# Joining the key loads of three head pairs and copying a quarter half aside

## The chip, the cores and the metric

The kernel runs on one core of a Trainium2 chip. The metric is the device time of one execution in microseconds (us), as the median of several runs; lower is better. All times here are microseconds unless marked ns. Engine names are those of the profile: PE (TensorE), DVE (VectorE), ACT (ScalarE), POOL (GpSimd), SP (the queue that issues almost all transfers).

## The reference

One decode step of a transformer block: attention over a long cache, then a small MLP mixer. What matters here is the attention, whose cache is nearly all of the data:

```
x: [1, 1, 512]; k_cache, v_cache: [1, 8, 16384, 128]; 32 query heads, 8 key/value heads, all bf16
q = (layernorm(x) @ wq) as 32 heads of 128
scores = q . k * 128**-0.5      (4 query heads share one key head)
p = softmax(scores);  o = p @ v;  h = x + o @ wo
out = h + B(layernorm(h))       (B: layernorm, two small branches, gelu with w3 and w4)
```

With one position, the branch of B that shifts along the sequence contributes nothing, so w1 and w2 are not read; w3 and w4 are.

## The kernel before, in words

The key and the value cache are 33.6 MB each. The kernel walks over four **pairs** of key/value heads (`PAIRS = 4`, loop at L720). For a pair, each of the 128 partitions holds 256 cache rows of 128 numbers: 64 KB of keys and 64 KB of values, 8.4 MB over all partitions. There is one key buffer `kb_all` and one value buffer `vb` of that size, so a pair's data can only be loaded when the pair before has been read. The key buffer is used as two **halves**, `kb[0]` and `kb[1]` (L444), 32 KB a partition each.

Per pair:
- `clear` (L658, ACT) zeroes the score banks; L724 (DVE) copies the pair's queries to `qn`.
- For each half y, `transpose_keys` (L635, DVE) transposes the half from `kb[y]` into the buffer `kt`. A half has eight **pieces**; `cuts` says at which pieces an instruction starts: (0, 4) is two instructions of four pieces, (0, 1, 2, 4, 6) five of 1, 1, 2, 2, 2. Both halves use the same `kt`, so a piece of the second half can only be written when PE has read that piece of the first.
- `scores` (L646, PE) does four matmuls a piece into the score banks. PE waits for DVE piece by piece.
- `load_keys(j + 1, y)` (L465, SP) loads the half of the next pair into `kb[y]`, once DVE has read it.
- `softmax` (L662): maximum (DVE, L664), a small matmul (L667), the exponential (ACT, L675), and the transposes of the probabilities into `pt` (DVE, L679).
- `unread(16)` (L498, matmuls of L500) lets PE do matmuls whose result nobody reads, while it waits for the softmax.
- `values` (L682): 64 matmuls with the values as the moving operand; they need `pt` and the landed values. `gather` (L700) rescales and adds up the output (L706 to L714). Then `load_values(j + 1)` (L470) loads the next pair's values into `vb`.

Every transfer is issued from SP in the order of the program, so SP's order is wq (two loads), keys 0 (two halves), values 0, keys 1 (two), values 1, keys 2 (two), values 2, keys 3 (two), values 3, then the weights: wo (L743, two loads, into `kb[0]`), w3 (L747) and w4 in three loads (L750), both into `kb[1]`. Each waits on SP for its buffer. One DMA semaphore per name (`k0`, `k1`, `v`, ...) counts a load's landing, and a reader waits for the whole load.

After the last pair the attention output is multiplied with wo (L759), the second layernorm follows on DVE (L514 to L561, inverse roots without ACT), then w3 (L784), GELU (ACT, L796), transposes (L800), w4 (L807), the output casts (L814 on DVE, L815 on ACT) and the store (L817).

PE's program is a hand-built loop over pieces and pairs, with one wait on DVE's count per piece; `worth` in an operation is by how much it raises that count (the number of pieces of a transpose).

Of the kernel before, what the change touches and what calls it, by code (L numbers as in the profile page):

```python
# [7 lines left out]
BF16 = mybir.dt.bfloat16  # L8
I32 = mybir.dt.int32
# [341 lines left out]
NHC = FM // 128  # L351

WQ = 2048
WO = ((0, 20), (20, 32))
VP = 1

# [3 lines left out]
PAIRS = HKV // 2  # L360
RPARTS = 6
QPAD = 4 * 7
KP = 8 * DH
# [9 lines left out]
def bass_sequential_preLN__gqa_block_cached__mixer_s_mlp__decode_kernel(  # L373
# [13 lines left out]
    with ExitStack() as ctx:  # L387
        sb = lambda name, shape, dt: ctx.enter_context(nc.sbuf_tensor(name, shape, dt))
        ps = lambda name, shape, dt: ctx.enter_context(nc.psum_tensor(name, shape, dt))
        P = Program(nc, ctx)  # L390
# [52 lines left out]
        kb_all = sb("kb", [128, 256 * DH], BF16)  # L443
        kb = [kb_all[:, i * 128 * DH:(i + 1) * 128 * DH] for i in range(2)]  # L444
        vb = sb("vb", [128, 256 * DH], BF16)
        kt = sb("kt", [128, 128 * DH], BF16)
        wq_sb, wo_sb = vb, kb[0]
        w3_sb = kb[1][:, 0:NCH * FM].rearrange("p (k f) -> p k f", k=NCH)
        w4_sb = kb[1][:, NCH * FM:2 * NCH * FM].rearrange("p (m c) -> p m c", m=NHC)
# [9 lines left out]
        def load(name, dst, src, key, by="SP", also=()):  # L459
            P.op(by, lambda e: e.dma_start(dst, src), w=[key, *also], dma=name)  # L460

        def pair_rows(src, j):
            return src[0, 2 * j:2 * j + 2].rearrange("g (u t) d -> (g u) (t d)", u=64)

        def load_keys(j, y):  # L465
            n = 128 * DH
            load(f"k{y}", kb[y][:, :], pair_rows(A_k_cache, j)[:, y * n:(y + 1) * n], ("r", y, 0),
                 also=[("r", y, i) for i in range(1, RPARTS)])

# [15 lines left out]
        def dve(fn, r=(), w=(), bank=()):  # L485
            return P.op("DVE", fn, r, w, bank)

        def act(fn, r=(), w=(), bank=()):
            return P.op("ACT", fn, r, w, bank)
# [8 lines left out]
        def unread(times):  # L498
            field = qb[:, :, :, :].rearrange("p a j q -> p (a j q)")
            P.op("PE", lambda e: e.matmul(O_ps[1][:, :], field[:, 0:128], field[:, 0:512], start=True, stop=True),  # L500
                 r=["qb"], bank=[("O", 1)], times=times)

        def piece(cuts, m):
            return [lo <= m < hi for lo, hi in cuts].index(True)
# [42 lines left out]
        def inverse_roots(i, ns):  # L547
# [23 lines left out]
        load("wq0", wq_sb[:, 0:WQ], wq_in[:, 0:WQ], "wq0")  # L571
        load("wq1", wq_sb[:, WQ:NCH * HQ * DH], wq_in[:, WQ:NCH * HQ * DH], ("v", 0), also=[("v", x) for x in range(1, VP)])
        load_keys(0, 0)
        load_keys(0, 1)

        dve(lambda e: e.memset(mean4[:, :], -1.0 / (32 * D)), w=["mean4"])
        pool(lambda e: e.memset(ident_f[:, :], 0.0), w=["ident_f"])
# [6 lines left out]
            r=["ident_f", "x4"], w=["quarter"])  # L584
# [11 lines left out]
            r=["ident_f"], w=["row32"])  # L596
        dve(lambda e: e.tensor_reduce(maskdd[:, :], ident_f[:, :].rearrange("p (n d) -> p d n", d=4), AX.X, ALU.add),
            r=["ident_f"], w=["maskdd"])
# [3 lines left out]
        for z, src, key, of, n in ((zo, row32[:, :].rearrange("p (g n h) -> p g h n", g=2, h=REP), "zo", "row32", 4),  # L602
# [6 lines left out]
            r=["hT", (("st", 0), 0), (("st", 0), 6), "wq0"] + [("v", x) for x in range(VP)], w=["xn"])  # L609
# [3 lines left out]
        for i, key in enumerate(keys):  # L613
            P.part("query", i)
            for k in range(NCH):
                pe(lambda e, k=k: e.matmul(row[:, bass.ds(P.b + P.b0, 512)], copies(xn[:, k:k + 1], 128),  # L616
                                           wq_k[:, k, bass.ds(P.c + P.c0, REP * DH)], start=(k == 0), stop=(k == NCH - 1)),
                   r=["xn"], also=[("v", x) for x in range(VP)], w=["n" if key == "mn" else key], bank=[key])
        P.part()
        for g in range(2):  # L620
            half = banks[64 * g:64 * g + 64, PAIRS * g:PAIRS * g + PAIRS, :].rearrange("p j c -> p (j c)")
            for b in range(2):
# [3 lines left out]
                    r=["n" if x == "mn" else x for x in keys[PAIRS * g:PAIRS * g + PAIRS]], w=["qcol"],  # L626
# [5 lines left out]
                qcol[lo:hi, :, :, 0].rearrange("p n (j h) -> p n j h", h=REP)), r=["qcol"], w=["qb"])  # L632


        def transpose_keys(y, cuts):  # L635
            for t, n in zip(cuts, [b - a for a, b in zip(cuts, [*cuts[1:], 8])]):
                view = lambda x, t=t, n=n: x[:, :].bitcast(I32).rearrange("p (x l w) -> p x (l w)", x=2, l=64)[
                    :, :, t * 512:(t + n) * 512]
                P.op("DVE", lambda e, view=view: e.transpose(view(kt), view(kb[y])),  # L639
                     r=[("r", y, i) for i in range(RPARTS)], w=[("kt", t + i) for i in range(n)], worth=n)  # L640

        def key_piece(at, n):
            part = kt[:, :].rearrange("p (x f) -> p x f", x=2)[:, :, bass.ds(at, KP)]
# [76 lines left out]
        for j in range(PAIRS):  # L720
            P.part()
            clear()
            P.part("query", j)
            dve(lambda e, j=j: e.tensor_copy(qn[:, :, :], qb[:, :, j, :]), r=["qb", ("s", 0), ("s", 1)], w=["qn"])  # L724
            for y in range(2):
                P.part("half", j, y)
                transpose_keys(y, (0, 4) if j < PAIRS - 1 else range(8) if y else (0, 1, 2, 4, 6))
                scores(j, y)
                if j < PAIRS - 1:
                    load_keys(j + 1, y)  # L730
            P.part("middle", j)
            softmax(j)
            unread(16)
            sums(j)
            values(j)
            P.part("rest", j)
            gather(j)
            if j < PAIRS - 1:
                load_values(j + 1)
# [9 lines left out]
        for n, (lo, hi) in enumerate(W4):  # L749
# [4 lines left out]
            r=["o_m"], w=["o_f"])  # L754
        dve(lambda e: e.tensor_copy(o_b[:, :], o_f[:, :]), r=["o_f", ("r", 0, 0)], w=["o_b"])  # L755

        for r_ in range(32):
# [4 lines left out]
               r=["o_b"] + [("r", 0, n) for n in (piece(WO, r_),) if n], w=[("O", 0)], bank=[("O", 0)],  # L762
# [4 lines left out]
        for n in range(2):  # L767
            dve(lambda e, n=n: e.tensor_copy(osum[:, 256 * n:256 * n + 256], O_ps[0][:, 256 * n:256 * n + 256]),
                r=[("O", 0)], w=[("osum", n)], bank=[("O", 0)])
        for q in range(4):  # L770
            pe(lambda e, q=q: e.matmul(h_ps[32 * q:32 * q + 32, 0:128], copies(row32[:, 0:1], 32),
                                       osum[:, q * 128:(q + 1) * 128], start=True, stop=True),
               r=[("osum", q // 2), "row32"], w=[hkey], bank=[hkey])
# [4 lines left out]
            r=["hT", (S, 0)] + [("r", 1, 0)], w=["hc"])  # L778
# [3 lines left out]
        for k in range(NCH):  # L782
            for q in range(4):
                pe(lambda e, k=k, q=q: e.matmul(s_ps[32 * q:32 * q + 32, 0, 0:FQ], hc[:, k, :],  # L784
                                                w3_sb[:, k, q * FQ:(q + 1) * FQ], start=(k == 0), stop=(k == NCH - 1)),
                   r=["hc"] + [("r", 1, n) for n in (piece(W3, k),) if n], w=[("s", 0)], bank=[("s", 0)])
# [6 lines left out]
            r=["xs", (S, 6), "hr"], w=[hkey], bank=[hkey])  # L793
# [9 lines left out]
        for m in range(NHC):  # L803
            if m == 4:
                pe(None)
            for o in range(4):
# [3 lines left out]
                   r=[("hcol", 2 * m // NHC)] + [("r", 1, len(W3) + n) for n in (piece(W4, m),) if n],  # L810
                   w=[hkey], bank=[hkey])
# [7 lines left out]
             r=[("fin", 0), ("fin", 1)], w=["out"], dma="out")  # L819
# [32 lines left out]
```

## Time and profile before

| | us |
|---|---|
| time, median of 3 runs (lowest to highest) | 189.69 (189.59 to 189.78) |
| span of the profiled execution | 189.0 |
| PE / DVE / ACT busy | 128.6 / 116.8 / 13.7 |
| data moved | 79.19 MB, mean 419 GB/s over the span |

The span runs from the first to the last instruction of one profiled execution; the time of a run also holds what lies around it. In the rows of the profile a group is named by line, engine, operation, output<-input and count; the brackets in a timeline row give the idle time of the engine before the group and what ended it. "kb" is the key buffer, which the wo, w3 and w4 loads use later.

### The profile page before, as it was taken

The numbers are of one execution on the slowest core, as the hardware profiler recorded it, in microseconds if no ns is written. First come the engines' busy times: TensorE is split into PE (matmuls) and PEld (weight loads), VectorE is DVE, ScalarE is ACT, GpSimd is POOL, SyncE is SP. The second block draws the span as 40 slices with busy tenths as digits, with TensorE's granted clock in tenths as the row PEclk, the third lists the DMA queues.
The fourth block names the chain that finished last, engine by engine and source line by source line (L and its number), as shares of the span: only waits on it lengthen the run. The fifth ranks groups of instructions, "written<-read, shape, count | busy, mean of one in ns | idle before, by whom it ended". The sixth has DMA issues, their size and how long they took to land.

```text
span 189.0 us, 2407 instructions
## 1 busy us (share of the span) xinstructions
PE 128.6 (68%) x767; PEld 49.7 (26%) x767; DVE 116.8 (62%) x139; ACT 13.7 (7%) x21; POOL 4.6 (2%) x8
## 2 busy tenths in 40 slices
PE   0109804979699049796980597969829997885772
PEld 0103301423225014232250242322513332222221
DVE  5740699695350897954518969445179897523173
ACT  3000200000040000000400000004000000500012
POOL 8100000000000000000000000000000000000000
PEclk9999995899999958999998589999987999999999
DMA  6999999999799999997999999997999999799994
GB/s 239 455 416 444 444 444 444 444 444 444 340 437 444 444 555 444 416 416 305 416 444 444 409 479 444 444 444 333 444 444 437 520 416 416 333 429 427 431 412 178
DMA packets 2895, 79.19 MB, mean 419 GB/s; under 512 B 334, under 2 KB 462, under 8 KB 718
## 3 DMA queue, kind: packets, MB, share of 16 engines
q1 hardware_dynamic: 2886, 79.17, 97.9%
q8 instruction: 1, 0.02, 0.0%
q10 hardware_dynamic: 8, 0.00, 0.0%
HBM read 79.17 MB, written 0.00 MB: 419 GB/s over the span
## 4 chain that ended last, share of the span: by engine, by line
DMA 36%; DVE 29%; PE 29%; issue 4%; SPq 1%; DVEq 0%
DVE kt L639 24%; DMA kb<-in_A_k_cache_dram 15%; DMA kb<-in_B_w_dram 15%; PE banks L650 13%; DMA vb<-in_A_wq_dram 6%; PE banks L500 6%; PE banks L616 5%; PE banks L690 4%; DVE mx L664 1%; DVE od L709 1%; DVE qcol L623 1%; SPq L460 1%; PE banks L667 1%; PE banks L712 0%; DVE od L706 0%
## 5 line engine op out<-in xcount | busy, mean ns | idle before, releaser
L650 PE MATMUL banks<-kt,qn 128*128 x256 | 69.2, 411 | 26.7 <-DVE kt L639 25.9
L639 DVE STREAM_TRANSPOSE kt<-kb 128x4096 int32<-128x4096 int32 (+2 forms) x25 | 70.7, 2878 | 5.6 <-PE banks L650 4.3
L650 PEld LDWEIGHTS banks<-kt,qn 128*128 x256 | 26.1, 102 | 69.2 <-issue 53.4
L500 PE MATMUL banks<-qb 128*128 128x512 bf16 x70 | 25.5, 388 | 0.6
L690 PE MATMUL banks<-vb,pt 128*32 128x512 bf16 x256 | 14.7, 379 | 0.9 <-POOLq L482 0.9
L675 ACT ACTIVATE p_sb<-banks,bias 128x1024 bf16<-128x1024 f32 x4 | 4.5, 1113 | 132.9 <-DVE nmh L671 132.9
L664 DVE TENSOR_REDUCE mx<-banks 128x1 f32<-128x1024 f32 x4 | 4.9, 1224 | 14.2 <-PE banks L650 14.2
L616 PE MATMUL banks<-vb,xn 128*128 x32 | 8.9, 448 | 6.8 <-DVE xn L607 6.8
L679 DVE STREAM_TRANSPOSE pt<-p_sb 64x1024 bf16<-64x1024 bf16 x8 | 9.9, 1239 | 5.4 <-ACT p_sb L675 5.3
L500 PEld LDWEIGHTS banks<-qb 128*128 128x128 bf16 x70 | 6.7, 97 | 18.3 <-issue 18.1
L706 DVE TENSOR_SCALAR od<-banks,rowc 128x128 f32<-128x128 f32 x4 | 1.4, 351 | 14.4 <-PE banks L690 14.4
L690 PEld LDWEIGHTS banks<-vb,pt 128*32 128x32 bf16 x256 | 8.5, 97 | 5.2 <-POOLq L482 1.0
L623 DVE STREAM_TRANSPOSE qcol<-banks 64x1024 f32<-64x1024 f32 x4 | 4.8, 1228 | 7.1 <-PE banks L616 7.1
L616 PEld LDWEIGHTS banks<-vb,xn 128*128 128x128 bf16 x32 | 3.6, 111 | 11.7 <-issue 9.2
L667 PE MATMUL banks<-mxd,mean 128*128 128x128 f32 x8 | 2.0, 326 | 6.6 <-DVE mxd L665 6.6
L712 PE MATMUL banks<-od,zo 128*32 128x128 f32 x8 | 1.6, 285 | 6.5 <-DVE od L709 6.5
L659 ACT ACTIVATE banks<-mean 128x1024 f32<-128x1024 f32 x4 | 4.1, 1027 | 19.0 <-DVE qcol L623 18.9
L699 DVE RECIPROCAL den<-banks 32x1 f32<-32x1 f32 x4 | 0.6, 156 | 6.9 <-PE banks L697 6.9
L709 DVE SCALAR_TENSOR_TENSOR od<-banks,rowc,od 128x128 f32<-128x128 f32 x12 | 4.2, 351 | 0.4
L759 PE MATMUL banks<-kb,o_b 128*32 128x512 bf16 x44 | 3.3, 384 | 1.6 <-DVE o_b L755 1.1
L585 PE MATMUL banks<-x,quarter 4*128 4x128 bf16 x1 | 0.3, 281 | 5.4 <-DVE quarter L583 5.4
L583 DVE CAST quarter<-ident_f 4x128 bf16<-4x128 f32 x1 | 3.2, 3225 | 1.0 <-DMA x<-in_A_x_dram 1.0
(69 smaller groups left out, 39.6 us busy)
## 6 DMA issues: line engine op xcount, KB each, us to landing
kb<-in_A_k_cache_dram SPq DMA_DIRECT2D x8, 4096.0 KB, 27.6
vb<-in_A_wq_dram SPq DMA_DIRECT2D x1, 3584.0 KB, 11.7
kb<-in_A_wo_dram SPq DMA_DIRECT2D x1, 2560.0 KB, 26.1
kb<-in_B_w_dram SPq DMA_DIRECT2D x1, 1792.0 KB, 24.2
kb<-in_A_wo_dram SPq DMA_DIRECT2D x1, 1536.0 KB, 29.4
kb<-in_B_w_dram SPq DMA_DIRECT2D x1, 1024.0 KB, 26.3
kb<-in_B_w_dram SPq DMA_DIRECT2D x1, 640.0 KB, 27.4
vb<-in_A_wq_dram SPq DMA_DIRECT2D x1, 512.0 KB, 3.6
```

Source lines behind the costliest of these rows:

```text
L500: P.op("PE", lambda e: e.matmul(O_ps[1][:, :], field[:, 0:128], field[:, 0:512], start=True, stop=True), r=["qb"], bank=[("O", 1)], times= ...
L616: pe(lambda e, k=k: e.matmul(row[:, bass.ds(P.b + P.b0, 512)], copies(xn[:, k:k + 1], 128), wq_k[:, k, bass.ds(P.c + P.c0, REP * DH)], sta ...
L623: dve(lambda e, g=g, b=b, half=half: e.transpose(qcol[64 * g:64 * g + 64, 2 * b:2 * b + 2, :, :].rearrange("p e m u -> p (e m u)"), half.r ...
L639: P.op("DVE", lambda e, view=view: e.transpose(view(kt), view(kb[y])), r=[("r", y, i) for i in range(RPARTS)], w=[("kt", t + i) for i in r ...
L650: pe(lambda e, n=n: e.matmul(row[:, bass.ds(P.y, 512)], qn[:, n, bass.ds(P.q, 128)], key_piece(P.k, n), start=False, stop=(n == 3), skip_g ...
L659: act(lambda e: e.activation(s_all, copies(mean4[:, 0:1], 1024), ACTF.Identity, scale=0.0), r=["mean4", "p"], w=[("s", 0), ("s", 1)], **both)
L664: dve(lambda e: e.tensor_reduce(mx[:, :], s_all, AX.X, ALU.max), r=[("s", 0), ("s", 1)], w=["mx"], **both)
L667: pe(lambda e: e.matmul(m_ps[:, 0:128], mean4[:, :], mxd[:, :], start=True, stop=True), r=["mxd", "mean4"], w=["m"], bank=["mn"])
L675: act(lambda e: e.activation(p_sb[:, :], s_all, ACTF.Exp, bias=bias[:, 0:1], scale=float(SCALE), accum_out=acc[:, :]), r=[("s", 0), ("s", ...
L679: dve(lambda e, g=g: e.transpose(pt[64 * g:64 * g + 64, :, :, g, :], p_sb[64 * g:64 * g + 64, :]), r=["p"], w=["pt"])
L690: pe(lambda e, l=l, ct=ct, ch=ch: e.matmul(O_ps[0][32 * ct:32 * ct + 32, :], pt[:, l, ch, :, :].rearrange("p g u -> p (g u)"), tiles[:, l ...
L709: dve(lambda e, block=block, c=c: e.scalar_tensor_tensor(od[:, :], block, rowc[:, c:c + 1], od[:, :], ALU.mult, ALU.add), r=[key, "rowc", ...
```

## The change

The keys of pairs 0, 1 and 2 (`WHOLE = 3`) come in one load each, 64 KB a partition, into the whole of `kb_all`; pair 3 keeps its two halves. The next pair's joined load is issued after the second half's scores are set up, and it waits for every reader of both halves. So that it need not wait for the last transposes, ACT copies the last two pieces (`ASIDE = 2`) of the second half into a new buffer `aside` as soon as the keys have landed, and DVE transposes those two pieces from there. The cuts change: for pairs 0 to 2 the first half goes in 2, 2, 4 pieces and the second in 4, 2, 2; for pair 3 the first half goes in 2, 2, 4 (1, 1, 2, 2, 2 before) and the second in eight single pieces as before. `unread` does 13 matmuls instead of 16, in all four pairs.

```diff
+WHOLE, ASIDE = 3, 2
...
+        aside = sb("aside", [128, 2, ASIDE * KP], BF16)
...
         def load_keys(j, y):
             n = 128 * DH
+            if j < WHOLE:
+                load("k0", kb_all[:, :], pair_rows(A_k_cache, j), ("r", 0, 0),
+                     also=[("r", 0, i) for i in range(1, RPARTS)] + [("r", 1, i) for i in range(RPARTS)])
+                return
             load(f"k{y}", kb[y][:, :], pair_rows(A_k_cache, j)[:, y * n:(y + 1) * n], ("r", y, 0),
...
         load_keys(0, 0)
-        load_keys(0, 1)
...
+        def pieces(x, t, n):
+            return x[:, :].rearrange("p (x l) -> p x l", x=2)[:, :, t * KP:(t + n) * KP]
+
+        def put_aside():
+            act(lambda e: e.copy(aside[:, :, :], pieces(kb[1], 8 - ASIDE, ASIDE)),
+                r=[("r", 1, i) for i in range(RPARTS)], w=["aside"])
+
-        def transpose_keys(y, cuts):
+        def transpose_keys(y, cuts, from_aside=False):
             for t, n in zip(cuts, [b - a for a, b in zip(cuts, [*cuts[1:], 8])]):
-                view = lambda x, t=t, n=n: x[:, :].bitcast(I32).rearrange("p (x l w) -> p x (l w)", x=2, l=64)[
-                    :, :, t * 512:(t + n) * 512]
-                P.op("DVE", lambda e, view=view: e.transpose(view(kt), view(kb[y])),
-                     r=[("r", y, i) for i in range(RPARTS)], w=[("kt", t + i) for i in range(n)], worth=n)
+                of = aside[:, :, :] if from_aside and t == 8 - ASIDE else pieces(kb[y], t, n)
+                P.op("DVE", lambda e, of=of, t=t, n=n: e.transpose(pieces(kt, t, n).bitcast(I32), of.bitcast(I32)),
+                     r=["aside"] if from_aside and t == 8 - ASIDE else [("r", y, i) for i in range(RPARTS)],
+                     w=[("kt", t + i) for i in range(n)], worth=n)
...
             dve(lambda e, j=j: e.tensor_copy(qn[:, :, :], qb[:, :, j, :]), r=["qb", ("s", 0), ("s", 1)], w=["qn"])
+            if j < WHOLE:
+                put_aside()
             for y in range(2):
                 P.part("half", j, y)
-                transpose_keys(y, (0, 4) if j < PAIRS - 1 else range(8) if y else (0, 1, 2, 4, 6))
+                if j < WHOLE:
+                    transpose_keys(y, (0, 4, 8 - ASIDE) if y else (0, 2, 4), from_aside=y == 1)
+                else:
+                    transpose_keys(y, range(8) if y else (0, 2, 4))
                 scores(j, y)
-                if j < PAIRS - 1:
+                if j < PAIRS - 1 and (y or j + 1 >= WHOLE):
                     load_keys(j + 1, y)
             P.part("middle", j)
             softmax(j)
-            unread(16)
+            unread(13)
```

On SP the joined load of pairs 1 and 2 stands where the second half's load stood; the first half's load, which was issued between the halves, is gone. For pair 3 both halves are issued where they were. On ACT the copy stands between `clear` and the exponential of pairs 0 to 2.

## The prediction

> **What bounds the kernel now.** The page first: span, transfer queue, chain.
>
> ```profile
> span 189.0 us, 2407 instructions
> ...
> q1 hardware_dynamic: 2886, 79.17, 97.9%
> ...
> DMA 36%; DVE 29%; PE 29%; issue 4%; SPq 1%; DVEq 0%
> ```
>
> The transfer engines are busy for 97.9% of the span, so the 79 MB of loads set a floor and the engines work beside them. The span is 189.0; the median of the runs, 189.69, lies 0.7 above it, and I keep that 0.7 as what lies around the span.
>
> Next, when each load lands. The timeline of SP's queue gives the issue times, the page's view of transfers, asked for each issue's window, the time from issue to landing.
>
> ```profile
> 1.65 1.02 SPq L460 DMA_DIRECT2D kb<-in_A_k_cache_dram  x2
> 22.83 0.33 SPq L460 DMA_DIRECT2D vb<-in_A_v_cache_dram  x1
> 35.16 10.53 SPq L460 DMA_DIRECT2D kb<-in_A_k_cache_dram  x2
> 61.46 0.33 SPq L460 DMA_DIRECT2D vb<-in_A_v_cache_dram  x1
> ...
> 82.92 0.33 SPq L460 DMA_DIRECT2D kb<-in_A_k_cache_dram  x1
> ```
>
> ```profile
> kb<-in_A_k_cache_dram SPq DMA_DIRECT2D x1, 4096.0 KB, 30.2
> vb<-in_A_v_cache_dram SPq DMA_DIRECT2D x1, 28.9
> kb<-in_A_k_cache_dram SPq DMA_DIRECT2D x1, 4096.0 KB, 26.2
> kb<-in_A_k_cache_dram SPq DMA_DIRECT2D x1, 4096.0 KB, 25.8
> vb<-in_A_v_cache_dram SPq DMA_DIRECT2D x1, 29.1
> kb<-in_A_k_cache_dram SPq DMA_DIRECT2D x1, 4096.0 KB, 27.4
> vb<-in_A_wq_dram SPq DMA_DIRECT2D x1, 512.0 KB, 3.6
> ```
>
> A merged row ends with its last issue of 0.33, so the second key half of pair 0 goes out at 1.65 + 1.02 - 0.33 = 2.34 and lands at 2.34 + 30.2 = 32.5. In the same way: values of pair 0 at 51.7; key halves of pair 1 at 61.4 and 45.36 + 25.8 = 71.2; values of pair 1 at 90.6; second key half of pair 2 at 82.92 + 27.4 = 110.3. Loads land one behind the other; every load is issued long before the one ahead of it ends.
>
> Then what one pair costs the engines (pair 2 and the start of pair 3).
>
> ```profile
> 101.40 8.76 DVE L639 STREAM_TRANSPOSE kt<-kb 128x4096 int32<-128x4096 int32 x2
> 111.60 8.77 DVE L639 STREAM_TRANSPOSE kt<-kb 128x4096 int32<-128x4096 int32 x2 [1.43 <-PE banks L650]
> ...
> 124.68 1.22 DVE L664 TENSOR_REDUCE mx<-banks 128x1 f32<-128x1024 f32 x1 [4.31 <-PE banks L650]
> ...
> 128.65 2.49 DVE L679 STREAM_TRANSPOSE pt<-p_sb 64x1024 bf16<-64x1024 bf16 x2 [1.33 <-ACT p_sb L675]
> ...
> 136.35 0.35 DVE L706 TENSOR_SCALAR od<-banks,rowc 128x128 f32<-128x128 f32 x1 [3.35 <-PE banks L690]
> ...
> 138.74 0.32 DVE L724 COPY qn<-qb 128x624 bf16<-128x624 bf16 x1
> 139.59 8.95 DVE L639 STREAM_TRANSPOSE kt<-kb 128x1024 int32<-128x1024 int32 x5 [0.53 <-DMA kb<-in_A_k_cache_dram]
> ...
> 149.30 9.13 DVE L639 STREAM_TRANSPOSE kt<-kb 128x1024 int32<-128x1024 int32 x8 [0.76 <-DMA kb<-in_A_k_cache_dram]
> ```
>
> Pair 2 transposes from 101.4, although its second key half lands only at 110.3: the engines start each pair on its first half, ahead of the transfers. They need 139.06 - 101.4 = 37.6 a pair against some 39.1 for its 16.8 MB (71.2 to 110.3), and reach pair 3 half a microsecond before its first half lands (139.59). Only there, and at the end, do engines wait for data.
>
> The end of the timeline:
>
> ```profile
> 159.68 1.22 DVE L664 TENSOR_REDUCE mx<-banks 128x1 f32<-128x1024 f32 x1 [1.25 <-PE banks L650]
> ...
> 172.41 0.35 DVE L706 TENSOR_SCALAR od<-banks,rowc 128x128 f32<-128x128 f32 x1 [4.41 <-PE banks L690]
> ...
> 175.43 2.54 PE L759 MATMUL banks<-kb,o_b 128*32 128x512 bf16 x32 [1.05 <-DVE o_b L755]
> ...
> 178.46 0.83 PE L759 MATMUL banks<-kb,o_b 128*32 128x512 bf16 x12 [0.48 <-DMA kb<-in_A_wo_dram]
> ...
> 183.86 0.16 DVE L561 SCALAR_TENSOR_TENSOR st<-st,sti 128x2 f32<-128x2 f32 x1
> 184.24 0.85 ACT L796 ACTIVATE hg<-banks,st 128x224 bf16<-128x224 f32 x2 [0.76 <-PE banks L784]
> 185.28 1.05 DVE L800 STREAM_TRANSPOSE hcol<-hg 128x224 bf16<-128x224 bf16 x2 [0.78 <-DMA kb<-in_B_w_dram]
> ...
> 186.83 0.56 PE L807 MATMUL banks<-kb,hcol 128*32 128x128 bf16 x24 [0.20 <-DMA kb<-in_B_w_dram]
> 187.44 0.28 DVE L814 CAST fin<-banks 64x128 bf16<-64x128 f32 x1 [1.11 <-PE banks L807]
> ```
>
> From the end of the wo matmuls (178.46 + 0.83 = 179.29) everything is one chain that waits for weights at two places by tenths only. Its own length: to the inverse root 184.02 - 179.29 = 4.73; 0.2 until the GELU starts; half of its 0.85; the transposes 1.05; 28 of the last matmuls, some 0.65. That is 7.1, where 187.44 - 179.29 = 8.15 passed. So the engines have **1.05 of slack** against the loads at the end, no more.
>
> **The change part by part.** *The joined load.* One semaphore now speaks for both halves, so the first transpose of pairs 0 to 2, and on DVE the whole pair behind it, waits for the second half: pair 0 from its present start of 26.3 (behind the query) to 32.5, pair 2 from 101.4 to 110.3. SP issues two instructions fewer before values 0 and one fewer before values 1 and 2; none of those waits on them. Rows of 64 KB instead of 32 KB: keys took 71.2 - 51.7 = 19.5 and 110.3 - 90.6 = 19.7, values (already 64 KB a row) 51.7 - 32.5 = 19.2 and 19.4. The gain lies between nothing and 0.5 a load; the means differ by 0.3, with single landings scattering as much, so I take 0.2: 0.6 by pair 2. Its keys then land at **109.7**.
>
> *Release of the buffer.* The next pair's keys go out after the transpose of the second half's third quarter (pieces 4 and 5) and ScalarE's copy of its last. A four-piece transpose takes 4.4 by the row at 101.40; for two pieces and for the copy I use these groups:
>
> ```profile
> L639 DVE STREAM_TRANSPOSE kt<-kb 128x2048 int32<-128x2048 int32 x3 | 6.7, 2269 | 0.0
> ...
> L659 ACT ACTIVATE banks<-mean 128x1024 f32<-128x1024 f32 x4 | 4.1, 1027 | 19.0 <-DVE qcol L623 18.9
> ```
>
> The copy has 4096 elements a partition, so it lies between one L659 and four, 1.0 to 4.1; I take 4.1, since it moves four times the elements. It starts at the landing; the next thing on ScalarE is the exponential some 23 later. It ends 11 before DVE reaches the release and costs nothing; it would from 15 on.
>
> *The new cuts*, timed from the start u of a pair's transposes. PE's pace, from the chain, the timeline and the stretches:
>
> ```profile
> 106.02 5.46 PE banks L650 x16
> ```
>
> ```profile
> 120.54 4.11 PE L650 MATMUL banks<-kt,qn 128*128 x16 [0.21 <-DVE kt L639]
> ...
> 126.61 6.03 PE L500 MATMUL banks<-qb 128*128 128x512 bf16 x16
> ```
>
> ```profile
> 105.00:108.00 3.00, 1.98 (x5) 0.81 (x6) 3.00 (x2) 0.00 (x0) 0.00 (x0) 0.50 0.81 350
> ```
>
> Four pieces (16 matmuls) take 4.11, or 5.46 just after the long wait, where the granted clock is 0.50.
> - First half in 2, 2 and 4 pieces: DVE ends at 2.27 + 2.27 + 4.4 less overlaps, 8.85 (four-four takes 8.76, the finer cut at 139.59 8.95). PE now starts at u + 2.4 instead of u + 4.6 and has done four pieces at 2.4 + 5.5 = 7.9. DVE needs just those to be free, so its stall of 1.43 goes. PE takes pieces 4 to 7 from 9.0 to 13.1.
> - Second half: 8.85 + 4.4 = 13.25, release at 15.5, last piece from the side buffer at 17.7. What is late next is PE: eight pieces from 13.4 at 1.03 each, scores done at **u + 21.6**, against 124.68 - 101.49 = 23.2 now. Finer cuts at the end of the half bring nothing more.
> - Three warming matmuls fewer: 3 x 6.03 / 16 = 1.13. They end at 132.64 now, the transposed probabilities are there at 128.65 + 2.49 = 131.14, so all 1.13 counts.
> - From scores to the next pair's start 139.06 - 124.68 = 14.4 now, 13.25 then. A pair takes 21.6 + 13.25 = **34.85** instead of 37.6.
>
> *Does the queue stay full?* Pair 0 starts at 32.3, gives its buffer free at 47.8 and is done at 67.2. Pair 1 starts with its keys at 70.8, releases at 86.3, is done at 105.6. The wq row above (512 KB in 3.6, of which 1.2 is moving bytes at the values' 19.4 per 8.4 MB) gives at most 2.4 from issue to bytes at both ends. Values 0 land at 51.7 and values 1 at 90.2, so the keys have 1.5 to spare both times. Values of pairs 1 to 3 go out at u + 32.4, at least 3 before the keys ahead of them land.
>
> *The sum.* Pair 2 starts at 109.7 (8.3 later) and is done at 109.7 + 34.85 = 144.55. Keys of pair 3, still in halves, have landed by then (139.5 and 149.3 before), so pair 3 starts 5.0 later than at 139.59. Its first half again ends at u + 8.85; PE, empty from 7.9 to 9.0, then has twelve pieces in a row, 12.35 long, while DVE's eight single transposes take 9.13: scores done at u + 21.35 = 165.9, before 159.68. To the rescaling of the output 11.67 (136.35 - 124.68, with no wait for values) less 1.13: 176.45 against 172.41; here the wait for the last values has hidden part. Then 3.02 to wo and, with all of wo long landed, 2.54 + 0.83 = 3.37: wo ends at 182.85 against 179.29. The tail's own 7.1 leads to 189.95, where the output cast stood at 187.44. **+2.5**, a span of 191.5 and a time of 192.2.
>
> So the cover of the joined load is the start on half a pair: once it is gone, no pair can begin before its last byte, and from 109.7 on two pairs and the tail stand one behind the other, 80.2 long, where the loads after that point need only some 77.
>
> *A rule beside it.* The Trainium skill, TensorE: Matmul & The Clock Gate, in its part on the clock gate, says that the activity window is free-running and the number of slow matmuls changes from run to run. This trace has one phase only (the 0.50 row). By that rule PE could stay slow for up to two windows of 3.4 after its first matmul, an estimate from that page; four pieces would then end at u + 9.3 instead of 7.9.
>
> Apart from it, four pieces wholly at half clock (twice 4.11) would end at u + 10.6, a stall of 1.8 at most in pair 2; I take none, as the chain shows 5.46, and keep part of it in the range.
>
> **The rivals.**
> - *A dry queue.* If the copy does not free the buffer sooner (the change doesn't do what it says), release comes at u + 17.7: 50.0 and 88.5, about 0.7 inside the 2.4 each time. Keys 1 and 2 are late by 0 to 0.7 each, and pair 2 with them: 192.2 to 193.6. Against it: the copy's 4 lies far before 15.
> - *Faster, by fewer transfers.* If each load had a cost of its own of x that the next load does not cover, three joins bring pair 2's keys 3x earlier. 2.5 must be won over the 0.6 counted, so it decides from x = 1.0; at 2.4, the bound from the wq row, pair 2 starts at 103.1 and the time is 185.6. For it: nothing. Against it: halves land 71.2 - 61.4 = 9.8 apart, twice which is 19.6, and a single load of the same bytes takes 19.4.
>  The Trainium skill, DMA: Bandwidth & Descriptors, Anatomy of one DMA, gives each transfer a fixed cost of about 2.0; taken as x it would make an estimate of 186.8. The trace's 0.2 speaks against that for queued loads.
> - *Hidden anyway.* If the engines' chain were 2.5 shorter than summed (twenty matmul pieces at 0.9, say), the last weights would set the end again: 189.1 to 189.7. Pieces of 1.03 in every full-clock stretch speak against it.
>
> **How the numbers follow.** Forecast 0.79, own range 191.0 (0.4 a load) to 193.4 (no gain from longer rows, part of the slow-clock stall); dry queue 0.11; fewer transfers 0.04; hidden anyway 0.05, mostly within 0.2%; other 0.01. 0.2% is about what a measurement of this kernel can tell from no change. Predicted 192.2; range 190.9 to 194.2 (up to a dry queue with no gain from the rows), which leaves out the faster cases. Faster 0.06, same 0.04, slower 0.90.
>
> **What would show it.** Right: first transposes of pairs 0, 1 and 2 each right after a wait for keys, at about 32.3, 70.8 and 109.7; pair 3 waiting for PE's gather, not for data, near 144.5; no DVE wait on PE between the halves; the tail without waits for weights, its transfers done before its matmuls ask for them. Wrong: a transfer gap at 51 or 90 (dry queue), pair 2's keys before 107 (fewer transfers), or a last wait for w4 (hidden).

## The result and the profile after

The changed kernel takes **194.82** (median of 6 runs, 193.24 to 195.23) against 189.74 before (189.53 to 190.0): a ratio of **1.0259**, 95% interval 1.0241 to 1.0276. Ratios here and below are estimated over the runs and are not exactly the quotient of the two medians. The forecast was 192.2 with a range to 194.2; the direction and the path were right, but the forecast +2.5 is about half of the measured 5.1.

The page of the changed kernel, first its span, the transfer queue and the chain, then two groups (line, engine, operation, output<-input, count | busy, mean ns | idle before and its cause):

```profile
span 193.5 us, 2365 instructions
...
q1 hardware_dynamic: 2454, 79.17, 95.4%
...
DMA 40%; DVE 29%; PE 26%; issue 3%; SPq 0%; ACT 0%; DVEq 0%; ACTq 0%
DMA kb<-in_A_k_cache_dram 40%; DVE kt L650 23%; PE banks L662 13%; PE banks L506 5%; PE banks L702 4%; PE banks L776 2%; DVE mx L676 1%; DVE od L721 1%; PE banks L824 1%; PE banks L679 1%; PE banks L724 0%; SPq L462 0%; DVE od L718 0%; DVE hcol L817 0%; DVE mxd L677 0%
...
L650 DVE STREAM_TRANSPOSE kt<-kb 128x2048 int32<-128x2048 int32 (+2 forms) x26 | 63.9, 2524 | 14.3 <-DMA kb<-in_A_k_cache_dram 14.3
...
L644 ACT COPY aside<-kb 128x4096 bf16<-128x4096 bf16 x3 | 10.8, 3605 | 34.2 <-DMA kb<-in_A_k_cache_dram 34.2
```

The same bytes are moved, but the queue no longer fills the span (95.4% instead of 97.9%): the transfers are done before the end, and the last load of the weights is gone from the chain. It now runs through keys and transposes only. DVE waits 14.3 for keys, three times, where it waited 1.3 before. The copy takes 3.6 each time.

DVE's timeline, cut down to the points that the forecast named (start, duration, what ended the idle time before):

```profile
32.50 15.35 DVE L650 STREAM_TRANSPOSE kt<-kb 128x2048 int32<-128x2048 int32 x5 [5.72 <-DMA kb<-in_A_k_cache_dram]
...
72.00 15.39 DVE L650 STREAM_TRANSPOSE kt<-kb 128x2048 int32<-128x2048 int32 x5 [4.73 <-DMA kb<-in_A_k_cache_dram]
...
110.74 15.35 DVE L650 STREAM_TRANSPOSE kt<-kb 128x2048 int32<-128x2048 int32 x5 [3.84 <-DMA kb<-in_A_k_cache_dram]
...
132.31 1.23 DVE L676 TENSOR_REDUCE mx<-banks 128x1 f32<-128x1024 f32 x1 [4.03 <-PE banks L662]
...
145.38 17.84 DVE L650 STREAM_TRANSPOSE kt<-kb 128x2048 int32<-128x2048 int32 x11
...
166.90 1.22 DVE L676 TENSOR_REDUCE mx<-banks 128x1 f32<-128x1024 f32 x1 [3.68 <-PE banks L662]
...
177.35 0.35 DVE L718 TENSOR_SCALAR od<-banks,rowc 128x128 f32<-128x128 f32 x1 [3.35 <-PE banks L702]
...
191.98 0.28 DVE L831 CAST fin<-banks 64x128 bf16<-64x128 f32 x1 [0.68 <-PE banks L824]
```

Each joined pair begins right behind its wait for keys, the half-to-half stall on PE is gone (five transposes in a row), pair 3 waits for no data, and nothing in the tail waits for weights. Pair 2 starts 9.3 later than before (110.74 against 101.4) and everything behind it follows.

### The profile page after: what moved, and what is told of

Its sections match the earlier page's. It is cut to its first block, busy times and chain, and to the rows that moved or that the text cites. A ratio compares the mean times of both kernels' runs of the same rounds, so it can differ in the third digit from the quotient of the medians.

```text
span 193.5 us, 2365 instructions
## 1 busy us (share of the span) xinstructions
PE 127.6 (66%) x755; PEld 50.1 (26%) x755; DVE 116.8 (60%) x143; ACT 24.5 (13%) x24; POOL 4.6 (2%) x8
## 3 DMA queue, kind: packets, MB, share of 16 engines
q1 hardware_dynamic: 2454, 79.17, 95.4%
## 4 chain that ended last, share of the span: by engine, by line
DMA 40%; DVE 29%; PE 26%; issue 3%; SPq 0%; ACT 0%; DVEq 0%; ACTq 0%
DMA kb<-in_A_k_cache_dram 40%; DVE kt L650 23%; PE banks L662 13%; PE banks L506 5%; PE banks L702 4%; PE banks L776 2%; DVE mx L676 1%; DVE od L721 1%; PE banks L824 1%; PE banks L679 1%; PE banks L724 0%; SPq L462 0%; DVE od L718 0%; DVE hcol L817 0%; DVE mxd L677 0%
## 5 line engine op out<-in xcount | busy, mean ns | idle before, releaser
L662 PE MATMUL banks<-kt,qn 128*128 x256 | 71.7, 417 | 34.4 <-DVE kt L650 34.2
L650 DVE STREAM_TRANSPOSE kt<-kb 128x2048 int32<-128x2048 int32 (+2 forms) x26 | 63.9, 2524 | 14.3 <-DMA kb<-in_A_k_cache_dram 14.3
L506 PE MATMUL banks<-qb 128*128 128x512 bf16 x58 | 21.4, 425 | 0.4
L644 ACT COPY aside<-kb 128x4096 bf16<-128x4096 bf16 x3 | 10.8, 3605 | 34.2 <-DMA kb<-in_A_k_cache_dram 34.2
L702 PEld LDWEIGHTS banks<-vb,pt 128*32 128x32 bf16 x256 | 9.3, 97 | 3.4
L506 PEld LDWEIGHTS banks<-qb 128*128 128x128 bf16 x58 | 5.7, 99 | 15.0 <-issue 14.8
L650 DVE STREAM_TRANSPOSE kt<-aside 128x2048 int32<-128x2048 int32 x3 | 6.8, 2269 | 0.0
L671 ACT ACTIVATE banks<-mean 128x1024 f32<-128x1024 f32 x4 | 4.1, 1027 | 19.4 <-DVE qcol L628 19.3
L776 PE MATMUL banks<-kb,o_b 128*32 128x512 bf16 x44 | 4.5, 530 | 1.1 <-DVE o_b L772 1.1
```

The costliest lines, as they stand in the source:

```text
L644: act(lambda e: e.copy(aside[:, :, :], pieces(kb[1], 8 - ASIDE, ASIDE)), r=[("r", 1, i) for i in range(RPARTS)], w=["aside"])
L650: P.op("DVE", lambda e, of=of, t=t, n=n: e.transpose(pieces(kt, t, n).bitcast(I32), of.bitcast(I32)), r=["aside"] if from_aside and t == 8 ...
L662: pe(lambda e, n=n: e.matmul(row[:, bass.ds(P.y, 512)], qn[:, n, bass.ds(P.q, 128)], key_piece(P.k, n), start=False, stop=(n == 3), skip_g ...
L702: pe(lambda e, l=l, ct=ct, ch=ch: e.matmul(O_ps[0][32 * ct:32 * ct + 32, :], pt[:, l, ch, :, :].rearrange("p g u -> p (g u)"), tiles[:, l ...
L776: pe(lambda e, r_=r_, q=q: e.matmul(O_ps[0][32 * q:32 * q + 32, :], copies(o_b[:, r_:r_ + 1], 32), wo_sb[:, r_ * D:(r_ + 1) * D], start=(r ...
```

## The experiments

All diffs are against the changed kernel unless said otherwise; the ratios are against the kernel before. The theory: a joined pair cannot start before its last byte, and behind pair 2's last byte two pairs and the tail stand in series. The rivals: a dry transfer queue, the copy, the new cuts or the fewer warming matmuls, the 64 KB rows.

### The changed kernel again (e1_again)

> The changed kernel once more, to see which of its pieces repeat. My theory: pair 2 starts when its joined keys have landed (110 to 111 in the profile) and from there the engines set the end; spans fall into two groups near 191.9 and 193.5, the longer when the wo matmuls run partly at half clock. Rival (a dry transfer queue): the keys of pair 1 land late by about 0.8 every time, with stretched packets at their start, and this is the larger part of the excess over the forecast.

194.71 (ratio 1.0258, 1.0240 to 1.0277). Pair 2 starts at 111.16, wo takes 4.47. In this repeat pair 1 starts at 71.50, earlier than in the first profile, and pair 2 later: the lateness is there in both, but not at the same load. The spans lie between 192.9 and 193.8 here, so these four do not fall into the two groups that were expected. Single shorter runs exist all the same: one of the six above has a span of 191.9, and e5, e8, e9 and e13 each have one or two that are 1.2 to 1.6 below the next of the same kernel. None of these is a profiled run, so what they save is not shown.

### Which join costs (e3_whole2, e13_join_pair2)

```diff
-WHOLE, ASIDE = 3, 2
+WHOLE, ASIDE = 2, 2
```

> Only the keys of pairs 0 and 1 are joined. My theory: pair 1 starts at 71 to 72, pair 2 right behind it at 106 (its first half landed at 100.5), pair 3 at 141, 1.5 later than before; the tail's 1.05 of slack takes most of it: 189.7 to 190.6, the upper end if wo runs at half clock. Rival (each joined load costs alike, 5.1 / 3): 193.1.

190.30 (1.0035, 1.0017 to 1.0054). Two of the three joins cost 0.6 together. DVE in this kernel:

```profile
106.15 17.83 DVE L650 STREAM_TRANSPOSE kt<-kb 128x2048 int32<-128x2048 int32 x11
...
140.74 17.83 DVE L650 STREAM_TRANSPOSE kt<-kb 128x2048 int32<-128x2048 int32 x11
```

Pairs 2 and 3 start without a wait for data, right behind the pair before, and 34.6 apart.

The other way round, only pair 2's keys are joined:

```diff
-            if j < WHOLE:
+            if j == 2:
                 load("k0", kb_all[:, :], pair_rows(A_k_cache, j), ("r", 0, 0),
...
         load_keys(0, 0)
+        load_keys(0, 1)
...
-                if j < PAIRS - 1 and (y or j + 1 >= WHOLE):
+                if j < PAIRS - 1 and (y or j + 1 != 2):
```

> Only the keys of pair 2 are joined; pairs 0 and 1 come in halves. Theory (only the last join counts, since two pairs and the tail stand behind it, while pairs 0 and 1 have four spare microseconds each): pair 2 at 110 to 111, time 193.6 to 195, nearly as with three joins. Rival (each join costs alike): 191.4.

193.45 (1.0174, 1.0132 to 1.0217; a little below the forecast's lower end), with pair 2 at 109.98:

```profile
109.98 8.83 DVE L651 STREAM_TRANSPOSE kt<-kb 128x2048 int32<-128x2048 int32 x3 [12.88 <-DMA kb<-in_A_k_cache_dram]
```

DVE, which had reached pair 2 at 97, stands 12.88 until the last byte. This one join costs 3.7 of the 5.1, the other two alone 0.6. (The two do not add up to 5.1: in e13 the keys of pair 2 go out at 77.85, long before the values ahead of them land, and come without the lateness that is shown further down.) The joins do not cost alike: what counts is how much work stands behind the joined bytes.

### Start on half a pair (e4_halves_late, e11_late_first)

```diff
             if j < WHOLE:
-                load("k0", kb_all[:, :], pair_rows(A_k_cache, j), ("r", 0, 0),
-                     also=[("r", 0, i) for i in range(1, RPARTS)] + [("r", 1, i) for i in range(RPARTS)])
+                for h in range(2):
+                    load(f"k{h}", kb[h][:, :], pair_rows(A_k_cache, j)[:, h * n:(h + 1) * n], ("r", h, 0),
+                         also=[("r", h, i) for i in range(1, RPARTS)])
                 return
```

> Keys of pairs 0 to 2 again in two loads with a semaphore each, but both issued at the joint late release, and the last two pieces still copied aside; DVE starts on the first half. My theory (the wait for the last byte costs): pair 0 starts at 26.8, pair 2 at its first half near 100.5, the time is 189.3 to 190.0. Rival (late issue, or the copy on ScalarE, costs): 192 to 195.

189.69 (1.0001, 0.9991 to 1.0011). The run was not quite what was meant: the first half's load waits only for its own readers and, for pair 1, went out at 35.8, not with the second. A second version holds both back by an instruction on SP that waits for every reader of the buffer:

```diff
             if j < WHOLE:
+                if j:
+                    P.op("SP", lambda e: e.nop(), w=[("r", h, i) for h in range(2) for i in range(RPARTS)])
+                for h in range(2):
+                    load(f"k{h}", kb[h][:, :], pair_rows(A_k_cache, j)[:, h * n:(h + 1) * n], ("r", h, 0),
+                         also=[("r", h, i) for i in range(1, RPARTS)])
                 return
```

> The same two loads, both issued only when the whole buffer is free, but DVE starts a pair on its first half. Theory (the wait for the last byte is the cost): pair 2 starts at its first half, near 100.3, and the time is 189.4 to 190.0. Rival (the late issue costs by itself): 191 or more.

189.60 (0.9996, 0.9986 to 1.0005), with every piece of the change but the join in place: the copy, the cuts, 13 matmuls, the joint release.

```profile
100.16 8.83 DVE L653 STREAM_TRANSPOSE kt<-kb 128x2048 int32<-128x2048 int32 x3 [3.07 <-DMA kb<-in_A_k_cache_dram]
...
138.96 8.83 DVE L653 STREAM_TRANSPOSE kt<-kb 128x2048 int32<-128x2048 int32 x3 [3.09 <-DMA kb<-in_A_k_cache_dram]
```

The pairs start with their first halves, ten before the joined load would have landed, and the loads set the end again. The shorter pairs (34.6 instead of 37.6) show as a wait of 3.1 for data, with another 0.9 between the halves, and gain nothing.

### The cuts and the matmuls without a join (e2_whole0, e12_before_cuts)

```diff
-WHOLE, ASIDE = 3, 2
+WHOLE, ASIDE = 0, 2
...
         load_keys(0, 0)
+        load_keys(0, 1)
```

> No load is joined and nothing is copied aside; the new cuts and the 13 warming matmuls stay. My theory: the join alone costs time, so the loads set the end again: 189.3 to 190.0, a pair 34.8 long, pair 3 waiting for its first half at about 139.5. Rival (the new cuts or the missing warming matmuls cost, by the clock or by more instructions): 191 or more.

191.88 (1.0120, 1.0103 to 1.0137), outside what the theory allowed. But its page begins

```profile
span 188.3 us, 2376 instructions
```

which is the span of the kernel before in its runs beside (188.1 to 188.8). The excess lies outside the span: 3.4 to 3.7 here, where every other kernel has 1.3 to 1.6. This run is also not quite what its expectation says: with `WHOLE = 0` every pair takes the cuts of pair 3, so all second halves go in eight single pieces. So the kernel before got the new cuts for pairs 0 to 2 ((0, 2, 4) and (0, 4, 6)), the new one for pair 3, and 13 matmuls:

```diff
-                transpose_keys(y, (0, 4) if j < PAIRS - 1 else range(8) if y else (0, 1, 2, 4, 6))
+                transpose_keys(y, ((0, 4, 6) if y else (0, 2, 4)) if j < PAIRS - 1 else range(8) if y else (0, 2, 4))
...
-            unread(16)
+            unread(13)
```

> The kernel before with the new cuts in all pairs and 13 warming matmuls; no join, no copy, no buffer for it. If the 2.2 that the version without any join took more than the kernel before lies in these cuts or in the fewer matmuls: 191 to 192 here too, with a span near 188.4. If it is a matter of that one program (its span was that of the kernel before, and the excess lay outside the span): 189.4 to 190.0.

189.64 (1.0000, 0.9989 to 1.0011). Cuts and matmuls cost nothing where the loads set the end. What lengthened that one program outside its span stays open.

### Is it one chain from pair 2 on? (e7_unread16)

```diff
-            unread(13)
+            unread(16)
```

> The changed kernel with 16 warming matmuls a pair instead of 13. My theory: from pair 2 on the engines are one chain, so it pays 1.13 twice, in pairs 2 and 3: 197.0. Rival (transfers set the end): no change, 194.8.

196.51 (1.0367, 1.0345 to 1.0389), 1.7 more than the changed kernel and not 2.2. The profile shows why:

```profile
110.10 15.35 DVE L650 STREAM_TRANSPOSE kt<-kb 128x2048 int32<-128x2048 int32 x5 [3.14 <-DMA kb<-in_A_k_cache_dram]
...
145.92 17.84 DVE L650 STREAM_TRANSPOSE kt<-kb 128x2048 int32<-128x2048 int32 x11
```

```profile
182.13 4.29 PE L776 MATMUL banks<-kb,o_b 128*32 128x512 bf16 x44 [1.05 <-DVE o_b L772]
```

Pair 2 happened to start at 110.10, 0.64 earlier. From there pair 2 takes 145.92 - 110.10 = 35.8 (34.6 with 13 matmuls), and pair 3 to its wo matmuls 182.13 - 145.92 = 36.2 (35.0). Both pay 1.2 in full: one chain.

### The buffer's release (e6_no_aside, e9_aside4, e10_late_wait)

```diff
-            if j < WHOLE:
-                put_aside()
...
-                    transpose_keys(y, (0, 4, 8 - ASIDE) if y else (0, 2, 4), from_aside=y == 1)
+                    transpose_keys(y, (0, 4, 8 - ASIDE) if y else (0, 2, 4), from_aside=False)
```

> The changed kernel without the copy aside: the last two pieces are transposed from the key buffer, so the next keys are issued 2.2 later (about 50.2 and 89.7). My theory: this is inside the time from issue to bytes, the queue runs dry twice, pair 2 starts 1.4 to 4 later: 196.2 to 199. Rival (the copy buys nothing, or costs): 194.8 or below.

Ratio 1.0387 (1.0325 to 1.0448), some 197, with single runs from 195.12 to 199.58. The profile is of the shortest of them:

```profile
50.29 0.33 SPq L462 DMA_DIRECT2D kb<-in_A_k_cache_dram  x1
```

```profile
112.21 17.54 DVE L650 STREAM_TRANSPOSE kt<-kb 128x2048 int32<-128x2048 int32 x6 [5.13 <-DMA kb<-in_A_k_cache_dram]
```

Without the copy the keys of pair 1 go out at 50.29 and pair 2 starts at 112.21, 1.5 later than in the changed kernel. The copy is worth its place. The other direction is four pieces aside:

```diff
-WHOLE, ASIDE = 3, 2
+WHOLE, ASIDE = 3, 4
...
-                of = aside[:, :, :] if from_aside and t == 8 - ASIDE else pieces(kb[y], t, n)
+                of = aside[:, :, (t - 8 + ASIDE) * KP:(t - 8 + ASIDE + n) * KP] if from_aside and t >= 8 - ASIDE else pieces(kb[y], t, n)
...
-                     r=["aside"] if from_aside and t == 8 - ASIDE else [("r", y, i) for i in range(RPARTS)],
+                     r=["aside"] if from_aside and t >= 8 - ASIDE else [("r", y, i) for i in range(RPARTS)],
...
-                    transpose_keys(y, (0, 4, 8 - ASIDE) if y else (0, 2, 4), from_aside=y == 1)
+                    transpose_keys(y, (0, 4, 6) if y else (0, 2, 4), from_aside=y == 1)
```

> The changed kernel with four pieces copied aside instead of two, so that the joined keys go out 2.3 earlier, near 45.5 and 85, some 6 ahead of the values before them landing. Theory (the stretched packets at the start of the joined keys, and with them a landing up to 0.8 late, come from an issue too short ahead): no stretched packets, keys 1 land at 70.9 to 71.3 and keys 2 at 109.8 to 110.3, time 193.6 to 194.3. Rival (the 64 KB rows or the join itself stretch them): unchanged, 194.7.

193.74 (1.0185, 1.0147 to 1.0224). Here are issue times on SP and the time from issue to landing, first for the changed kernel (values 0, keys 1, values 1, keys 2), then for this one (values 0, keys 1, keys 2):

```profile
23.21 0.33 SPq L462 DMA_DIRECT2D vb<-in_A_v_cache_dram  x1
47.91 0.33 SPq L462 DMA_DIRECT2D kb<-in_A_k_cache_dram  x1
64.75 0.33 SPq L462 DMA_DIRECT2D vb<-in_A_v_cache_dram  x1
87.45 0.33 SPq L462 DMA_DIRECT2D kb<-in_A_k_cache_dram  x1
```

```profile
vb<-in_A_v_cache_dram SPq DMA_DIRECT2D x1, 28.5
kb<-in_A_k_cache_dram SPq DMA_DIRECT2D x1, 24.0
vb<-in_A_v_cache_dram SPq DMA_DIRECT2D x1, 26.5
kb<-in_A_k_cache_dram SPq DMA_DIRECT2D x1, 23.2
```

```profile
22.30 0.33 SPq L462 DMA_DIRECT2D vb<-in_A_v_cache_dram  x1
45.80 0.33 SPq L462 DMA_DIRECT2D kb<-in_A_k_cache_dram  x1
...
84.08 0.33 SPq L462 DMA_DIRECT2D kb<-in_A_k_cache_dram  x1
```

```profile
vb<-in_A_v_cache_dram SPq DMA_DIRECT2D x1, 29.1
kb<-in_A_k_cache_dram SPq DMA_DIRECT2D x1, 25.0
kb<-in_A_k_cache_dram SPq DMA_DIRECT2D x1, 25.4
```

In the changed kernel values 0 land at 51.7 and the keys of pair 1 at 47.91 + 24.0 = 71.9, 20.2 behind them. Values 1 land at 64.75 + 26.5 = 91.25 and the keys of pair 2 at 87.45 + 23.2 = 110.65, 19.4 behind. In e9 values 0 and keys 1 land at 51.4 and 70.8, 19.4 apart, and pair 2's keys are there at 84.08 + 25.4 = 109.5. DVE starts pair 2 on them:

```profile
109.56 13.16 DVE L650 STREAM_TRANSPOSE kt<-kb 128x2048 int32<-128x2048 int32 x4 [4.02 <-DMA kb<-in_A_k_cache_dram]
```

The **lead** of a load is the time from its issue to the landing of the load ahead of it. With a lead of 5.6 the keys come in step, 19.4 behind; with 3.8 those of pair 1 come 0.8 late and those of pair 2 do not, and the page shows the queue busy throughout. The other profiles agree. Over all runs, five joined key loads with a lead of 5.6 or more land 19.35 to 19.4 behind the load ahead (e9, e13, e14); eleven with a lead of 3.4 to 3.9 land 19.4 to 20.3 behind (the two halves of e10 taken together); the two of e6, with leads of 1.2 and 1.6, land 20.5 and 20.8 behind. So a short lead can cost up to 0.9, but not every time. Is that the long rows? The next run has two loads of 32 KB rows, held back as in e11, with the first transposes waiting for both:

```diff
...
-                     r=["aside"] if from_aside and t == 8 - ASIDE else [("r", y, i) for i in range(RPARTS)],
+                     r=["aside"] if from_aside and t == 8 - ASIDE else [("r", y, i) for i in range(RPARTS)]
+                     + [("r", 1, 0)] * from_both,
...
-                    transpose_keys(y, (0, 4, 8 - ASIDE) if y else (0, 2, 4), from_aside=y == 1)
+                    transpose_keys(y, (0, 4, 8 - ASIDE) if y else (0, 2, 4), from_aside=y == 1, from_both=True)
```

> As the changed kernel, with the joined load as two loads of 32 KB rows, both issued only when the whole buffer is free (in the earlier run with two loads the first went out as soon as its own half was read, near 41), and the first transposes waiting for both. If the short lead stretches the first packets: stretched here too, keys 2 at 110.3 to 111.2, time 194.3 to 195. If the long rows do it: no stretch, keys 2 near 109.9, time 193.5 to 194.1.

195.10 (1.0297, 1.0249 to 1.0345). Both go out together, near the changed kernel's time, and pair 2 starts at 110.66: late here too, with short rows. The lead does it, not the rows.

```profile
48.21 0.80 SPq L462 DMA_DIRECT2D kb<-in_A_k_cache_dram  x2
```

```profile
110.66 15.35 DVE L653 STREAM_TRANSPOSE kt<-kb 128x2048 int32<-128x2048 int32 x5 [4.09 <-DMA kb<-in_A_k_cache_dram]
```

### Two halves, both waited for (e5_halves_wait)

This run has the two loads of e4, and its first transposes wait for both as in e10.

> As the changed kernel, but the joined load is two loads of 32 KB rows, issued back to back at the same place, and the first transposes wait for both. My theory (what costs is the wait for the second half, the length of the rows does next to nothing): as the changed kernel, 194.8, with 0 to 0.6 more. Rival (the joined transfer of 64 KB rows itself is slow to start): pair 1's keys land 0.8 earlier than in the changed kernel and the time is near 194.0 or below.

194.01 (1.0211, 1.0159 to 1.0262).

```profile
109.91 15.35 DVE L651 STREAM_TRANSPOSE kt<-kb 128x2048 int32<-128x2048 int32 x5 [4.04 <-DMA kb<-in_A_k_cache_dram]
```

These are the numbers that the rival had named: pair 1's keys land 0.9 earlier than in the changed kernel, and the time is near 194.0. But as in e4, the first half went out early (41.26), so the lead was long, which the expectation had not seen; e10, without that lead, decides for the lead and against the rows. Pair 2 starts 0.35 later than in e9. Of that, 0.27 is there at pair 0's keys already (they land at 32.32, in e9 at 32.05); from there to pair 2's keys the two kernels take 77.45 and 77.43, so behind pair 0 the long rows bring nothing that shows.

### The wo matmuls (e8_warm_wo, e14_lead_warm)

PE in the changed kernel, and the stretches around wo (busy times by engine, then the granted clock, transfer share, GB/s):

```profile
180.38 4.53 PE L776 MATMUL banks<-kb,o_b 128*32 128x512 bf16 x44 [1.05 <-DVE o_b L772]
```

```profile
178.62:182.03 3.41, 2.01 (x22) 0.68 (x26) 1.14 (x4) 0.00 (x0) 0.00 (x0) 1.00 0.98 416
182.03:185.44 3.41, 3.41 (x30) 1.11 (x22) 0.49 (x2) 0.00 (x0) 0.00 (x0) 0.50 0.97 401
```

The same 44 matmuls took 2.54 + 0.83 before. The granted clock is halved for 3.41, from the middle of them on. Unread matmuls go where PE waits for the rescaling:

```diff
             P.part("rest", j)
+            unread(4)
...
+        for n in range(2):
+            unread(None)
         for r_ in range(32):
```

> The changed kernel with four unread matmuls behind the values matmuls of each pair and two ahead of wo, in time where PE idles. My theory (the wo matmuls are slow because the granted clock falls to half after a stretch with little PE work): wo takes 3.4 instead of 4.5 and the time is 193.2 to 193.6. Rival (they are slow for another reason, or the clock falls at another place instead): 194.8 or above.

194.12 (1.0214, 1.0168 to 1.0261), above the interval that was named. The wo matmuls run without the slow stretch:

```profile
180.95 3.13 PE L779 MATMUL banks<-kb,o_b 128*32 128x512 bf16 x44 [0.52 <-DVE o_b L773]
```

But pair 2 started at 111.28 in this profile, 0.5 later than in the changed kernel, and took back part of the 1.4; another 0.2 lies outside the span. With both repairs, four pieces aside and these matmuls:

> The changed kernel with both repairs at once: four pieces copied aside (keys issued 2.3 earlier) and the unread matmuls around the last rescaling. If the short lead and the half clock under wo are the whole of what the forecast missed inside the span: pair 2 at 109.5 to 109.8, wo 3.1 to 3.2 long, a span of 191.0 to 191.4 and 192.3 to 192.9 as time. If something else costs too: a span of 192 or more.

193.00 (1.0167, 1.0137 to 1.0197), span 191.6, spans of all runs 191.2 to 191.6.

```profile
109.58 8.83 DVE L650 STREAM_TRANSPOSE kt<-kb 128x2048 int32<-128x2048 int32 x3 [3.95 <-DMA kb<-in_A_k_cache_dram]
...
190.10 0.28 DVE L834 CAST fin<-banks 64x128 bf16<-64x128 f32 x1 [0.68 <-PE banks L827]
```

Pair 2 comes at 109.58 and wo takes 3.13, as expected. The span is 0.2 above the upper end and the median 0.1, since pair 2 took 35.2 here instead of 34.6: its scores are done 0.3 later and the 13 unread matmuls of its softmax take 5.15 instead of 4.81, partly at half clock (0.50 from 136 to 138).

## Why the prediction was right in its path and wrong in its size

The chain was the one forecast, point by point (forecast, then measured in the profile of the changed kernel):

| | forecast | measured |
|---|---|---|
| start of pair 0 | 32.3 | 32.50 |
| start of pair 1 | 70.8 | 72.00 |
| start of pair 2 | 109.7 | 110.74 |
| scores of pair 2 done, from its start | 21.6 | 21.57 |
| pair 2 in all | 34.85 | 34.64 |
| scores of pair 3 done, from its start | 21.35 | 21.52 |
| from there to the rescaling | 10.54 | 10.45 |
| wo matmuls | 3.37 | 4.53 |
| from wo to the output cast | 7.1 | 7.07 |
| span | 191.5 | 193.5 |

- **The step that failed first: "does the queue stay full?"** It gave the keys "1.5 to spare both times". The releases came as computed, 15.4 and 15.45 behind the starts of pairs 0 and 1 against 15.5, and so did the lead, 3.8 against 3.9. But the bound of 2.4 from issue to bytes, taken from one small load, is not what a late load costs. It is the dry-queue rival in a mild form, and it went together with the forecast instead of against it. Pair 2 started **1.04** later than forecast. In this profile 0.8 of that is pair 1's keys, 20.2 behind values 0 instead of 19.4; the other 0.2 is scattered in tenths. Over several profiles pair 2 started between 110.1 and 111.3 with the short lead and at 109.56 and 109.58 with the long one (e9, e14).
- **The second: the tail's own time was taken from a profile with a full clock.** The wo matmuls cost 4.53 instead of 3.37, **1.16**. The rule on the clock gate was weighed for pair 2, where slow matmuls are hidden under DVE (21.57 confirms it), and not for wo, where nothing hides them. In 13 profiles without the extra matmuls, the changed kernel's among them, wo took 3.9 to 4.7 in all but one (e6, 3.19); with them 3.13 twice. Where the loads set the end (e4, e11, e12) the slow wo stands too and costs nothing.
 The full clock in the forecast's profile was luck. In every profile here, wherever the clock was read (from 20 on), its changes lie on a grid of 3.41, and the grid lies differently in each execution. In the twelve slow profiles the 3.41 ahead of the fall hold 0.7 to 2.0 of PE work. In e6, which has the same two pauses ahead of wo, the grid cuts them into stretches with 1.78 and 2.30 of work, and the clock stays at 1.00; in the kernel before they hold 1.60 and 2.48. The busy time alone does not give the limit, since 1.60 kept the clock and 2.01 lost it.
 The Trainium skill, TensorE: Matmul & The Clock Gate, clock gate part, gives half clock after at least one idle window of 3.4, in steps of such windows. The 3.41 at 0.50 agrees with the step; that the window ahead was idle does not: PE was busy for 2.01 of it.
- **The third: 0.7 around the span.** Nineteen runs of the kernel before, beside e1 to e4, have spans of 188.1 to 188.8 and 1.26 to 1.44 around them, as the changed kernel has (1.29 to 1.35). The profiled execution of before with its 189.0 was a long one, so the forecast put 0.6 too little around its span.
- **The 0.6 for longer rows** is not what the runs show, and the keys' 109.7 came out near the 109.5 of e9 and e14 by luck. The 0.2 at pair 0 has some support: its joined keys land at 32.05 to 32.36, its halves at 32.22 to 32.54. For the other 0.4, the forecast let 77.4 pass from pair 0's keys to pair 2's instead of the 77.8 in the profile of before. With a long lead, joined keys do take 77.4 (e9, e14), but halves take 77.45 to 77.6 (e2, e4, e5, e11, e12). Most of the 0.4 was that one long execution, not the rows.
- Its side estimate for a slow clock, u + 9.3, comes out at 9.9 when it is redone: a start at 2.4, then 4.11 of work and 3.4 lost. The sum did not use it.
- Right: the engines set the end (e7), the copy is hidden at 3.6 and needed (e6), the stall between the halves and 1.13 of warming are won in full and bring nothing where data is late (e11, e12), joins of pairs 0 and 1 are nearly covered (e3), and pair 3 waits for no data. The rival with a fixed cost per load is out: it needed 1.0 a load, but two loads (e5) and one (e9) take 77.45 and 77.43 from pair 0's keys to pair 2's, and the intervals of two held-back loads (e10, 1.0249 to 1.0345) and of one (the changed kernel, 1.0241 to 1.0276) overlap.

1.04 from the keys, 1.16 from wo, less 0.2 in between make the 2.0 inside the span; with 0.6 around it the 2.6 is complete. Removing the first two (e14) brings the span back to 191.6, where 191.5 was forecast, though partly because pair 2 was 0.4 longer there and wo 0.2 shorter than in the sum. Three things stay open: what e2 spends outside its span, what makes single runs 1.2 to 1.6 shorter, and why a load with 3.8 of lead comes late in some cases and in step in others while its queue looks full.

None of the variants beats the kernel before: those that start every pair on its first half end with the loads, at 189.6 to 189.7 (e4, e11, e12).

## What to carry to other kernels

A joined load has one semaphore, so its first byte is usable only when its last has landed: before joining two loads, ask which engine starts on the first half, and how much work stands in series behind the last join. Here the two early joins were nearly free (0.6), and the last one cost 3.7. And when a change uncovers a chain that transfers used to hide, price its matmuls by both clocks (3.13 and 4.53 for wo here), and its loads by their lead.

## What was not expected of the hardware

- A queue can be full and still deliver late. Keys issued 5.6, 3.8 and about 1.2 ahead of the landing of the load before them (e9, the changed kernel, e6) put the start of pair 2 at 109.56, 110.74 and 112.21. The middle lead costs between nothing and 0.9 a load.
 The Trainium skill, DMA: Bandwidth & Descriptors, Anatomy of one DMA, has a fixed cost of about 2.0, given for transfers on GpSimd's path; the loads here are issued from SP. A lead of 3.8 would have covered it, and did not always.
- The granted clock fell to 0.50 behind a stretch in which PE was busy for 2.01 of 3.41, part of it with matmuls of 32 columns. The changes of the clock lie on a grid of 3.41 that differs from one execution to the next, and the same pauses cost the clock in the changed kernel (2.01 of work between two points of the grid) and not in e6 (1.78 and 2.30).
- A program (e2) spent 3.4 to 3.7 outside its span where the others spend 1.3 to 1.6, the same in all its runs.
